# A fused transformer block on one core: weight tiles split, first loads spread, and chunk 0's sum over shifts moved from TensorE to VectorE

## The chip, the cores and the metric

The kernel runs on one core of a Trainium2 chip. Its engines are TensorE (PE in the profile; PEld is its weight load), VectorE (DVE), ScalarE (ACT), GpSimd (POOL) and SyncE (SP), which work side by side and wait for each other through semaphores; each takes its instructions in the order in which the program lists them. Loads and stores are issued by SP or ACT and run on the core's DMA engines. SBUF is the on-chip memory, PSUM holds eight banks of 128 x 512 float32 that TensorE writes. The metric is the time of one execution on the device in microseconds (us).

## The reference

One pre-norm block over 2048 tokens of width 512: attention over 8 dilated earlier positions, then a gated feed-forward part with ReLU.

```python
S, D, H, Dh, W, dil, F = 2048, 512, 32, 16, 8, 2, 1376
def attn(x, wqkv, wo):
    q, k, v = split(x @ wqkv)                      # 32 heads of 16
    idx = pos[:, None] - arange(W)[None, :] * dil  # 8 positions, 2 apart
    logits = einsum("bhsd,bhswd->bhsw", q, k[idx]) * Dh ** -0.5
    logits = where(idx >= 0, logits, -1e9)
    o = einsum("bhsw,bhswd->bhsd", softmax(logits), v[idx])
    return o.reshape(B, S, D) @ wo
def ffn(x, Wg, Wu, Wd):
    gate = x @ Wg
    return ((gate * (gate > 0)) * (x @ Wu)) @ Wd
h   = x + attn(layernorm(x))
out = h + ffn(layernorm(h))
```

## The kernel before

The tokens go through in four chunks of 512 (`tk`). Activations are kept transposed (feature on the partitions), so that a matmul takes weights as its stationary side and 512 tokens as its moving side.

For each chunk:

- layer norm: statistics (`xst`, L432, and `xag`, L435, on VectorE), inverse root by Ln and Exp on ScalarE (L445, L449), scaling (`xxn`: L472 on VectorE in chunk 0, L469 on ScalarE in chunks 1 to 3), transposes on TensorE (`xtp`, L479), copied from a bank by ScalarE (`xte`, L491);
- projections: 12 groups of four matmuls for q, k and v (`qkv0` to `qkv11`, L523), each evicted by ScalarE into `qT`, `kT` or `vT` (L531). In chunk 0 the first two groups are cut into halves of 256 tokens, so that they can start when half of the transposes are there;
- scores: VectorE multiplies q with four shifted views of k at a time (`pr`, L570, 128 x 4096 elements), TensorE sums over the features of a head with the 0/1 matrix `sel` (`sc`, L576), ScalarE takes the exponential (`ex`, L585), in chunk 0 VectorE masks the first positions (`mk`, L588);
- weights: TensorE spreads the eight exponentials over the features with `spread` (`bc`, L604), ScalarE evicts the eight (`be`, L611); the denominator goes through L618, Ln (L621) and Exp (L624);
- weighted sum: for each of four feature tiles VectorE multiplies the eight weights with eight shifted views of v (`mu`, L641, 128 x 4096), then the eight shifts are summed. In the chunks of `PESUM`, which is chunk 0 alone, TensorE does it: eight matmuls with the identity that accumulate in a bank (`ac`, L657), and VectorE scales from the bank (`om`, L661). In the other chunks VectorE adds in a tree of three steps of 2048, 1024 and 512 elements (`tree`, L644) and scales from SBUF (`om`, L648);
- output projection (`wo`, L679), residual and row sums on VectorE (`rs`, L684), second layer norm (L417, L423, L472, L479, L491);
- feed-forward: 22 groups of four matmuls for up and gate (`mm`, L706), evicted by ScalarE (`ue`, L710, and `ge`, L713), multiplied by VectorE (`gu`, L726), then 44 matmuls down (`dn`, L738), the residual (`o`, L742) and a store of 128 KB for each of four row blocks (`os`, L745).

Loads come first, in `setup`: x of chunk 0 in four tiles of 128 KB, two on SP's queue and two on ACT's; then, all on SP's queue, three column blocks of `wqkv` into one tile `wqkv_sb`, x of chunk 1, and the other weights. While they run, 42 matmuls on zeros (`NWARM`, L501) keep TensorE at work.

The order of all other work is set when the program is built. `Plan` collects steps with an engine, an assumed duration, what they wait for and the buffers they take, and `order` lists them: for each engine it finds the steps that could start first, and among those within 0.02 us of the earliest it takes the one with the lowest number in the table `PRIO` (one number for each kind of step and chunk). Steps of all four chunks compete, so projections of later chunks fill TensorE while VectorE works on an earlier one. The order is fixed then; on the chip an instruction only waits for what it needs. The whole x, q, k and hidden tiles share nine buffers (`quad`), products five (`big`), and all matmul outputs eight banks.

Of the kernel before, what the change touches and what calls it, by code (L numbers as in the profile page):

```python
# [8 lines left out]
P = 128  # L9
BF16 = mybir.dt.bfloat16  # L10
# [8 lines left out]
    "warm": (1781, 0, 0, 0),  # L19
    "xst": (1203, 746, 745, 1415),  # L20
    "xag": (-282, 1949, -30, 1438),
    "xrl": (1793, 1763, 1382, 1315),
    "xre": (-53, 1440, 163, 1147),
    "xxn": (801, 1624, 1811, 770),
    "xtp": (-311, 1713, 1279, 573),
    "xte": (-262, -229, 650, 168),
    "qkh0": (1179, 0, 0, 0),
    "qkv0": (397, 1785, 1908, 1357),
    "qe0": (1681, 1220, 1006, 2030),
    "qkh1": (1937, 0, 0, 0),  # L30
    "qkv1": (-27, 1273, 1437, 1309),
    "qe1": (1158, 1502, 1711, 1742),
    "qkv2": (1063, -98, 1193, 1055),
    "qe2": (781, 1293, 1295, 228),
    "qkv3": (732, 1300, 1292, 1219),
    "qe3": (1047, 1347, 1124, 896),
    "qkv4": (1595, 1124, 1549, 240),
    "qe4": (1361, 1357, 882, 377),
    "qkv5": (1414, 1504, 884, 1956),
    "qe5": (354, -58, 1194, 1406),  # L40
    "qkv6": (-356, 1429, 1321, 596),
    "qe6": (996, 1730, 953, 1406),
    "qkv7": (734, 1117, 606, 1375),
    "qe7": (-77, 202, 746, 1484),
    "qkv8": (1584, 1310, 2037, 1115),
    "qe8": (1117, 1084, 1067, 376),
    "qkv9": (711, 23, 593, 938),
    "qe9": (932, 1014, 1152, 1138),
    "qkv10": (1375, 756, 1239, 1096),
    "qe10": (-230, 1252, 1734, 1733),  # L50
    "qkv11": (1671, 1280, 1609, 1967),
    "qe11": (17, 943, 1110, 1362),
    "pr0": (-254, 1165, 1607, 1958),
    "sc0": (-324, 876, 1138, 1287),
    "ex0": (756, 972, 1285, 1085),
    "mk0": (547, 0, 0, 0),
    "pr1": (-47, 530, 999, 2004),
    "sc1": (617, 73, 326, 1774),
    "ex1": (372, 1285, 758, 1130),
    "mk1": (1051, 0, 0, 0),  # L60
    "bc0": (1062, 1244, 1300, 1122),
    "be0": (1138, 1158, 1341, 1095),
    "bc1": (42, 1057, 699, 929),
    "be1": (36, 1684, 1111, 1258),
    "den": (1604, 689, -310, 821),
    "dl": (1791, 1275, 1907, 595),
    "dr": (1335, 1273, 1312, 1699),
    "mu0": (-164, -38, 1183, 1122),
    "ac0": (56, 0, 0, 0),
    "om0": (1093, 1067, 1357, 1300),  # L70
    "mu1": (146, 1353, 1431, 1276),
    "ac1": (1364, 0, 0, 0),
    "om1": (687, 1400, 5, 1302),
    "mu2": (996, 993, 161, 1313),
    "ac2": (-37, 0, 0, 0),
    "om2": (785, 1737, 229, 1404),
    "mu3": (1280, 1240, 1405, 5),
    "ac3": (1975, 0, 0, 0),
    "om3": (1495, 1120, 1180, 231),
    "wo0": (228, 1102, 202, -356),  # L80
    "rs0": (1574, 927, -330, 1158),
    "wo1": (1121, 432, -275, 1193),
    "rs1": (1304, 181, -310, 593),
    "wo2": (-108, -249, 1343, 1034),
    "rs2": (1102, 163, 1048, 1339),
    "wo3": (1179, 946, 1316, 167),
    "rs3": (1309, 1400, 693, 397),
    "hnm": (-250, 1262, 1176, 1363),
    "hsq": (244, 1092, 14, 765),
    "hrl": (1322, 1782, 205, -102),  # L90
    "hre": (1117, 239, 1257, 1320),
    "hxn": (192, 17, 162, 1698),
    "htp": (1031, 1241, 533, 327),
    "hte": (2061, 57, 1584, 1212),
    "mm0": (1870, 1327, 1049, 757),
    "ue0": (1213, 766, -307, 1776),
    "ge0": (1785, -53, 998, 568),
    "gu0": (98, 592, 1451, 1946),
    "mm1": (1000, 1132, 1013, 1247),
    "ue1": (6, 374, 1115, 1933),  # L100
    "ge1": (635, 1100, 1018, 226),
    "gu1": (989, 1213, 146, 931),
    "mm2": (1019, -16, 1051, 872),
    "ue2": (1353, 1361, 1035, 904),
    "ge2": (1251, 1286, 793, 688),
    "gu2": (1674, 1276, 742, 1268),
    "mm3": (1242, 927, 374, 100),
    "ue3": (785, 1698, 41, 1846),
    "ge3": (991, 1869, 1151, 1243),
    "gu3": (1285, 1286, 1272, 1933),  # L110
    "mm4": (1260, 676, 54, 888),
    "ue4": (1, 902, 18, 940),
    "ge4": (1049, 146, 1335, 318),
    "gu4": (1374, 1154, 856, 885),
    "mm5": (1780, 1419, 1193, 1736),
    "ue5": (759, 76, 1742, -129),
    "ge5": (1330, 1083, 1583, 1674),
    "gu5": (1092, -159, 1003, 1066),
    "dn0": (1353, 675, 769, 1954),
    "o0": (-141, 1183, 625, 1829),  # L120
    "os0": (979, 146, 1064, 721),
    "dn1": (901, 1303, 1923, 1112),
    "o1": (1389, 1184, 1790, 188),
    "os1": (1494, 1548, -366, 994),
    "dn2": (1232, 1130, 1287, 1315),
    "o2": (1101, 851, 1278, 1314),
    "os2": (616, 850, 2, 961),
    "dn3": (1208, 1778, 1237, 1152),
    "o3": (743, 1756, 401, 205),
    "os3": (754, 1354, 604, 1066),  # L130
    "xnb": (0, -102, -111, -87),
    "tree0": (0, 621, 196, -129),
# [664 lines left out]
```

## Time and profile before

| | us |
|---|---|
| median of three runs (217.9, 217.58, 216.07) | 217.58 |
| the profiled execution | 216.77 |
| its span in the trace | 215.0 |
| warm-up matmuls, first to last | 0.99 to 5.26 |
| first transposes | 6.59 to 8.02 |
| last matmul ends | 211.66 |
| ScalarE busy | 140.9 |
| one projection or feed-forward group's eviction on ScalarE (L531), mean | 0.60 |
| copy of two transposed row blocks on ScalarE (L491), mean | 1.03 |

The span goes from the first to the last recorded instruction. A group's mean duration can be longer than the distance from one such instruction to the next, as the engines overlap the end of one with the start of the next: a 512-column matmul has a mean of 0.38 us, but eight follow each other in 1.73 us.

### The profile page before, as it was taken

What the parts mean: (1) busy time and instruction counts of PE and PEld (TensorE: products, weight loads), DVE (VectorE), ACT (ScalarE), POOL (GpSimd) and SP (SyncE); (2) the same over time, 40 slices, a digit from 0 to 9 for tenths busy, and PEclk for the clock granted to TensorE, in tenths of its full rate; (3) what the DMA queues carried; (4) which work ended last, traced back from release to release, by engine and by line L of the source; (5) the groups of instructions that cost most, each with busy time, mean ns of one, the idle gap of its engine ahead of it and who ended that gap; (6) DMA issues with size and microseconds to landing.
All of it is one profiled execution on the core that took longest, in us unless ns stands there. A gap on an engine that the chain in (4) does not pass through costs nothing.

```text
span 215.0 us, 3002 instructions
## 1 busy us (share of the span) xinstructions
PE 205.2 (95%) x1141; PEld 98.4 (46%) x1162; DVE 158.6 (74%) x240; ACT 140.9 (66%) x263; POOL 1.6 (1%) x13
## 2 busy tenths in 40 slices
PE   7499899999999999999999999999999999999993
PEld 7255335544455643444444444445444445444441
DVE  6454995999638999999999999849999536212331
ACT  2539979998798976757549662893666453666400
POOL 3000000000000000000000000000000000000000
PEclk9769999999999999999999999999999999999999
DMA  5999800000000000000002000000000000200011
GB/s 165 357 404 375 269 0 5 2 0 0 3 0 0 0 3 0 0 0 3 26 0 73 3 0 0 0 26 27 0 24 0 0 3 24 73 0 5 24 49 49
DMA packets 8670, 10.71 MB, mean 50 GB/s; under 512 B 496, under 2 KB 7504, under 8 KB 8656
## 3 DMA queue, kind: packets, MB, share of 16 engines
q1 hardware_dynamic: 8368, 10.26, 13.9%
q10 hardware_dynamic: 288, 0.26, 0.4%
q8 instruction: 9, 0.15, 0.3%
q14 instruction: 5, 0.04, 0.1%
HBM read 8.42 MB, written 2.10 MB: 49 GB/s over the span
## 4 chain that ended last, share of the span: by engine, by line
PE 91%; DMA 3%; ACT 2%; issue 1%; SPq 1%; DVE 0%; ACTq 0%
PE bank L706 35%; PE bank L523 21%; PE bank L738 18%; PE bank L679 6%; PE bank L576 4%; DMA wqkv_sb<-in_A_wqkv_dram 3%; PE bank L657 3%; PE bank L479 3%; PE bank L604 1%; ACT quad L491 1%; PE bank L618 1%; SPq L342 0%; ACT row L469 0%; DVE row L742 0%; ACT gr L713 0%
## 5 line engine op out<-in xcount | busy, mean ns | idle before, releaser
L523 PE MATMUL bank<-quad,wqkv_sb 128*128 128x512 bf16 (+1 forms) x193 | 45.9, 387 | 2.3 <-DMA wqkv_sb<-in_A_wqkv_dram 1.2
L706 PE MATMUL bank<-quad,wg_sb 128*128 128x512 bf16 (+1 forms) x175 | 45.0, 379 | 0.1
L706 PE MATMUL bank<-quad,wu_sb 128*128 128x512 bf16 (+1 forms) x171 | 44.6, 379 | 0.2
L641 DVE TENSOR_TENSOR big<-big,vT 128x4096 bf16<-128x4096 bf16 x16 | 36.1, 2284 | 6.1 <-ACT big L611 3.9
L738 PE MATMUL bank<-wd_sb,gT 128*128 128x512 bf16 (+1 forms) x170 | 39.2, 379 | 0.3
L570 DVE TENSOR_TENSOR big<-quad,kT 128x4096 bf16<-128x4096 bf16 x16 | 36.0, 2282 | 0.7 <-ACT quad L531 0.7
L710 ACT CAST up_sb<-bank 128x512 bf16<-128x512 f32 (+1 forms) x44 | 25.5, 590 | 15.4 <-PE bank L706 10.9
L713 ACT ACTIVATE gr<-bank 128x512 bf16<-128x512 f32 (+1 forms) x44 | 26.0, 598 | 14.7 <-PE bank L706 10.8
L523 PEld LDWEIGHTS <-wqkv_sb 128*128 128x128 bf16 x200 | 22.4, 117 | 23.7 <-issue 6.8
L706 PEld LDWEIGHTS <-wu_sb 128*128 128x128 bf16 (+1 forms) x176 | 17.5, 100 | 20.6 <-issue 0.4
L726 DVE TENSOR_TENSOR gT<-gr,up_sb 128x1024 bf16<-128x1024 bf16 (+1 forms) x24 | 15.2, 642 | 15.8 <-ACT gr L713 15.4
L706 PEld LDWEIGHTS <-wg_sb 128*128 128x128 bf16 (+1 forms) x176 | 17.3, 100 | 20.9 <-issue 1.5
L738 PEld LDWEIGHTS <-gT 128*128 128x128 bf16 (+1 forms) x176 | 16.8, 98 | 20.5 <-issue 0.7
L644 DVE TENSOR_TENSOR big<-big 128x2048 bf16<-128x2048 bf16 (+2 forms) x36 | 25.9, 772 | 0.0
L491 ACT COPY quad<-bank 128x1024 bf16<-128x1024 bf16 x16 | 16.0, 1025 | 6.1 <-PE bank L479 6.1
L742 DVE TENSOR_TENSOR row<-x_sm,bank 128x512 bf16<-128x512 bf16 x16 | 10.9, 684 | 11.7 <-PE bank L738 11.1
L611 ACT CAST big<-bank 128x512 bf16<-128x512 f32 x32 | 17.6, 605 | 2.7 <-PE bank L604 2.7
L423 ACT ACTIVATE row<-x_sm,mv 128x512 bf16<-128x512 bf16 x16 | 11.4, 716 | 6.7 <-DVE mv L417 6.6
L684 DVE SCALAR_TENSOR_TENSOR x_sm<-x_sm,bank 128x512 bf16<-128x512 bf16 x16 | 10.9, 685 | 6.3 <-PE bank L679 6.0
L679 PE MATMUL bank<-wo_sb,quad 128*128 128x512 bf16 x63 | 15.1, 379 | 0.1
L531 ACT CAST quad<-bank 128x512 bf16<-128x512 f32 x16 | 9.6, 598 | 5.6 <-PE bank L523 5.6
L432 DVE BATCH_NORM_STATS2 st<-x_sm 128x6 f32<-128x512 bf16 x16 | 10.1, 674 | 4.2 <-DMA x_sm<-in_A_x_dram 4.2
(53 smaller groups left out, 133.6 us busy)
## 6 DMA issues: line engine op xcount, KB each, us to landing
out_dram<-row SPq DMA_DIRECT2D x16, 128.0 KB, 1.7
wqkv_sb<-in_A_wqkv_dram SPq DMA_DIRECT2D x3, 512.0 KB, 6.2
x_sm<-in_A_x_dram SPq DMA_DIRECT2D x3, 512.0 KB, 14.0
wu_sb<-in_B_W_up_dram SPq DMA_DIRECT2D x1, 1376.0 KB, 10.8
wg_sb<-in_B_W_gate_dram SPq DMA_DIRECT2D x1, 1376.0 KB, 14.5
wd_sb<-in_B_W_down_dram SPq DMA_DIRECT2D x1, 1280.0 KB, 14.1
wo_sb<-in_A_wo_dram SPq DMA_DIRECT2D x1, 512.0 KB, 8.8
x_sm<-in_A_x_dram ACTq DMA_DIRECT2D x2, 128.0 KB, 2.9
```

Of the source, the lines that this page charges most:

```text
L491: nc.scalar.copy(out=dst.t[:, :, j0 * P:(j0 + n) * P], in_=i)
L523: nc.tensor.matmul(mm.t[:, lo:hi], lhsT=wqkv_sb[:, dt, c * D + t:(c + 1) * D:NT], rhs=xnT.t[:, dt, lo:hi], start=(dt == 0), stop=(dt == NT ...
L570: V.tensor_tensor(out=pb.t[:].rearrange("p (t w) s -> p t w s", t=2), in0=q4, in1=k4, op=ALU.mult)
L611: nc.scalar.copy(out=ab.t[:, w, :], in_=bc.t[:])
L641: V.tensor_tensor(out=mt.t[:], in0=ab.t[:], in1=v8, op=ALU.mult)
L644: V.tensor_tensor(out=mt.t[:, 0:n, :], in0=mt.t[:, 0:n, :], in1=mt.t[:, n:2 * n, :], op=ALU.add)
L679: nc.tensor.matmul(od.t[:], lhsT=OT.t[:, t, j * P:(j + 1) * P], rhs=wo_sb[:, t, :], start=(t == 0), stop=(t == NT - 1))
L706: nc.tensor.matmul(mm.t[:fs, :], lhsT=w_sb[:, dt, ft * P: ft * P + fs], rhs=hnT.t[:, dt, :], start=(dt == 0), stop=(dt == NT - 1))
L710: nc.scalar.copy(out=ub.t[:fs, i, :], in_=um.t[:fs, :])
L713: nc.scalar.activation(out=gr.t[:fs, i, :], in_=gm.t[:fs, :], func=ACT.Relu)
L726: V.tensor_tensor(out=gt.t[:fs, 0:n, :], in0=gr.t[:fs, 0:n, :], in1=ub.t[:fs, 0:n, :], op=ALU.mult)
L738: nc.tensor.matmul(od.t[:], lhsT=gts[ft].t[:fs, ft % 2, j * P:(j + 1) * P], rhs=wd_sb[:fs, ft, :], start=(ft == 0), stop=(ft == NFT - 1))
```

## The change

- The three column blocks of `wqkv` get tiles of their own, `wq_sb`, `wk_sb` and `wv_sb`. x of chunk 0 comes in two loads of 256 KB, one on each queue; then q on SP's queue, k on ACT's, v on SP's.
- `PESUM` is empty: the tree on VectorE sums the shifts in all four chunks.
- In chunk 0 the second half of the transposes is copied from its bank by VectorE instead of ScalarE.
- 54 warm-up matmuls instead of 42.
- In `order` the stretch within which a weightier step may be taken is 0.05 us for TensorE, 0.3 for VectorE and 0.1 for ScalarE instead of 0.02, and all of `PRIO` is replaced; assumed landing times of q, k and v change a little.
- A branch that transposes by DMA is added for the chunks in `DMAT`, of which there are none.

```diff
-    "mu0": (-164, -38, 1183, 1122),
-    "ac0": (56, 0, 0, 0),
+    "mu0": (-490, -741, -300, -559),
+    "tree0": (-169, -269, -240, -508),
...
+    LOOK = {"PE": 0.05, "DVE": 0.3, "ACT": 0.1}
...
-                    ((t, op) for t, op in cands if t <= first + 0.02),
+                    ((t, op) for t, op in cands if t <= first + self.LOOK.get(eng, 0.02)),
...
-    wqkv_sb = sb.tile([P, NT, 3 * D], BF16, name="wqkv_sb")
+    w3_sb = [sb.tile([P, NT, D], BF16, name=f"w{n}_sb") for n in "qkv"]
...
-        wq_r = A_wqkv.rearrange("(dt p) f -> p dt f", p=P)
-        nc.sync.dma_start(x_sm[:, 0:1, :], x_rows[:, 0:1, :])
-        nc.scalar.dma_start(x_sm[:, 1:2, :], x_rows[:, 1:2, :])
-        nc.sync.dma_start(x_sm[:, 2:3, :], x_rows[:, 2:3, :])
-        nc.scalar.dma_start(x_sm[:, 3:4, :], x_rows[:, 3:4, :])
-        for c in range(3):
-            nc.sync.dma_start(wqkv_sb[:, :, c * D:(c + 1) * D], wq_r[:, :, c * D:(c + 1) * D])
+        w3_r = A_wqkv.rearrange("(dt p) f -> p dt f", p=P)
+        nc.sync.dma_start(x_sm[:, 0:2, :], x_rows[:, 0:2, :])
+        nc.scalar.dma_start(x_sm[:, 2:4, :], x_rows[:, 2:4, :])
+        for c, q in enumerate((nc.sync, nc.scalar, nc.sync)):
+            q.dma_start(w3_sb[c][:], w3_r[:, :, c * D:(c + 1) * D])
         nc.sync.dma_start(x_sm[:, BPC:2 * BPC, :], x_rows[:, BPC:2 * BPC, :])
...
-    PESUM = (0,)
-    NWARM = 42
+    PESUM = ()
+    NWARM = 54
+    DMAT = ()
...
-             (("q", 6.0), ("k", 7.5), ("v", 9.0), ("o", 12.5), ("u", 16.5), ("g", 20.5), ("d", 28.0))}
+             (("q", 5.7), ("k", 7.0), ("v", 8.5), ("o", 12.5), ("u", 16.5), ("g", 20.5), ("d", 28.0))}
...
+                tev = not residual and tk == 0 and j0 > 0
...
+                    if tev:
+                        V.tensor_copy(out=o, in_=i)
+                    else:
+                        nc.scalar.copy(out=o, in_=i)
...
-                    nc.tensor.matmul(mm.t[:, lo:hi], lhsT=wqkv_sb[:, dt, c * D + t:(c + 1) * D:NT],
+                    nc.tensor.matmul(mm.t[:, lo:hi], lhsT=w3_sb[c][:, dt, t:D:NT],
...
-            if tk in PESUM:
+            if (tk, t) in PESUM:
```

Lines of the changed kernel are numbered otherwise: L429 and L432 are the statistics, L487 the scaling, L510 and L512 the copies of the transposes by VectorE and ScalarE, L552 the evictions of the projections, L591 the score products, L606 the exponentials, L632 the eviction of the weights, L662 the weighted products, L665 the tree, L669 the scaling after it, L705 the residual.

VectorE at the start of the program, before (`st` and `mv` hold the statistics, `row` a scaled row block):

```order
L432 BN_STATS st_113<-x_sm 128x6
L432 BN_STATS st_114<-x_sm 128x6
L435 BN_AGGR mv_117<-st_113 128x2
L432 BN_STATS st_115<-x_sm 128x6
L435 BN_AGGR mv_117<-st_114 128x2
L432 BN_STATS st_116<-x_sm 128x6
L435 BN_AGGR mv_117<-st_115 128x2
L435 BN_AGGR mv_117<-st_116 128x2
L472 TENSOR_SCALAR row_104<-x_sm,mv_117,rs_129 128x512
```

VectorE at the same place after the change, from the last statistics of chunk 0 to the first of chunk 1:

```order
L429 BN_STATS st_118<-x_sm 128x6
L432 BN_AGGR mv_119<-st_118 128x2
L487 TENSOR_SCALAR row_106<-x_sm,mv_119,rs_131 128x512
L487 TENSOR_SCALAR row_107<-x_sm,mv_119,rs_131 128x512
L487 TENSOR_SCALAR row_108<-x_sm,mv_119,rs_131 128x512
L487 TENSOR_SCALAR row_109<-x_sm,mv_119,rs_131 128x512
L510 COPY quad_80<-bank_137 128x4x256
L429 BN_STATS st_115<-x_sm 128x6
```

All four statistics still stand ahead of the first scaling; the copy of the second half is new on VectorE and stands ahead of chunk 1's statistics.

VectorE from chunk 0's weighted products on, before (`big` the products, `vT` and `kT` the values and keys, `bank` PSUM, `rec` the inverse denominators):

```order
L641 TENSOR_TENSOR big_87<-big_91,vT 128x4096
L453 SCALAR_TENSOR_TENSOR nb_126<-mv_120,rs_131 128x4
L641 TENSOR_TENSOR big_88<-big_91,vT 128x4096
L453 SCALAR_TENSOR_TENSOR nb_127<-mv_119,rs_132 128x4
L641 TENSOR_TENSOR big_89<-big_91,vT 128x4096
L641 TENSOR_TENSOR big_90<-big_91,vT 128x4096
L570 TENSOR_TENSOR big_87<-quad_81,kT 128x4096
L570 TENSOR_TENSOR big_88<-quad_81,kT 128x4096
L661 TENSOR_TENSOR quad_84<-bank_137,rec_103 128x512
L661 TENSOR_TENSOR quad_84<-bank_136,rec_103 128x512
```

The same place after the change:

```order
L662 TENSOR_TENSOR big_89<-big_93,vT 128x4096
L450 SCALAR_TENSOR_TENSOR nb_128<-mv_122,rs_133 128x4
L662 TENSOR_TENSOR big_90<-big_93,vT 128x4096
L662 TENSOR_TENSOR big_91<-big_93,vT 128x4096
L665 TENSOR_TENSOR big_90<-big_90 128x2048
L665 TENSOR_TENSOR big_90<-big_90 128x1024
L665 TENSOR_TENSOR big_90<-big_90 128x512
L662 TENSOR_TENSOR big_92<-big_93,vT 128x4096
L432 BN_AGGR mv_121<-st_118 128x2
L665 TENSOR_TENSOR big_89<-big_89 128x2048
L665 TENSOR_TENSOR big_89<-big_89 128x1024
```

Where chunk 1's score products followed the four weighted products, the trees of chunk 0 stand now; the score products come behind them.

ScalarE around the eviction of chunk 0's weights, before (`ex` the exponentials, `big_91` the weights):

```order
L585 ACTIVATE ex_100<-bank_135 128x512
L531 CAST vT<-bank_136 128x512
L611 CAST big_91<-bank_140 128x512
L611 CAST big_91<-bank_133 128x512
L531 CAST kT<-bank_138 128x512
L611 CAST big_91<-bank_134 128x512
L611 CAST big_91<-bank_135 128x512
L611 CAST big_91<-bank_136 128x512
L611 CAST big_91<-bank_140 128x512
L611 CAST big_91<-bank_133 128x512
L531 CAST vT<-bank_134 128x512
L611 CAST big_91<-bank_139 128x512
```

The same place after the change (`big_93` the weights):

```order
L606 ACTIVATE ex_102<-bank_142 128x512
L632 CAST big_93<-bank_139 128x512
L632 CAST big_93<-bank_140 128x512
L632 CAST big_93<-bank_136 128x512
L632 CAST big_93<-bank_141 128x512
L632 CAST big_93<-bank_135 128x512
L632 CAST big_93<-bank_142 128x512
L632 CAST big_93<-bank_139 128x512
L632 CAST big_93<-bank_140 128x512
L442 ACTIVATE rs_133<-mv_122,eps_t 128x4
```

Three evictions of projections stood between the exponential and the last of the eight; now the eight follow the exponential in one run.

249 lines of the change are left out of this document (130 added, 119 removed).

## The prediction

> **What bounds the kernel now.** I read the page first, then the chain of work that ended last, the groups by line, the timeline of TensorE and of VectorE over the first 100 us, and last the windows and the waits of VectorE.
>
> The page: its first line, TensorE's busy line, and the chain by engine; behind them, from the groups by line, the one that the change removes and the scaling that takes over for another (columns: line, engine, operation, count; busy us, mean ns; idle before).
>
> ```profile
> span 215.0 us, 3002 instructions
> PE 205.2 (95%) x1141; PEld 98.4 (46%) x1162; DVE 158.6 (74%) x240; ACT 140.9 (66%) x263; POOL 1.6 (1%) x13
> PE 91%; DMA 3%; ACT 2%; issue 1%; SPq 1%; DVE 0%; ACTq 0%
> L657 PE MATMUL bank<-big,identity 128*128 128x512 bf16 x31 | 7.5, 379 | 0.1
> ...
> L648 DVE TENSOR_TENSOR quad<-big,rec 128x512 bf16<-128x512 bf16 x12 | 4.9, 417 | 0.0
> ```
>
> TensorE is busy 95% of the span and is 91% of the chain. VectorE's 74% is a mean: by stage it is much fuller, as the windows below show. So work taken off TensorE shortens the span one for one only as long as VectorE does not fall behind it.
>
> The chain in order of time (start, length, what): the weights' load, eight of the matmuls that sum over shifts, the first output projection of chunk 1, the last VectorE step.
>
> ```profile
> 2.66 7.20 DMA wqkv_sb<-in_A_wqkv_dram
> ...
> 41.40 1.73 PE bank L657 x8
> ...
> 98.14 0.86 PE bank L679 x4
> ...
> 211.68 0.69 DVE row L742
> ```
>
> **Part 1, the sum over shifts in chunk 0.** The 32 matmuls of L657 go; eight take 1.73, so TensorE loses 32 x 0.216 = 6.9 us, all of it on the chain. VectorE takes over four trees of three adds. These rows of its timeline give the pitch of each step as the distance to the next row:
>
> ```profile
> 40.34 4.48 DVE L641 TENSOR_TENSOR big<-big,vT 128x4096 bf16<-128x4096 bf16 x2
> 44.74 4.48 DVE L570 TENSOR_TENSOR big<-quad,kT 128x4096 bf16<-128x4096 bf16 x2
> 49.14 1.88 DVE L661 TENSOR_TENSOR quad<-bank,rec 128x512 bf16<-128x512 f32 x3
> ...
> 71.01 4.23 DVE L644 TENSOR_TENSOR big<-big 128x2048 bf16<-128x2048 bf16 x6
> 75.15 4.49 DVE L570 TENSOR_TENSOR big<-quad,kT 128x4096 bf16<-128x4096 bf16 x2
> ```
>
> A product is (44.74 - 40.34) / 2 = 2.20; a tree is (75.15 - 71.01) / 2 = 2.07. The scaling that follows takes 0.42 from SBUF (L648 above), some 0.34 of it at the pitch of a full engine, where it was about 0.6 from a bank (three in 1.88). Net on VectorE: 4 x 2.07 - 4 x 0.27 = +7.2 us, all in chunk 0. The copy that evicts the second half of the first transposes also moves to VectorE (part 2).
>
> **Part 2, the start.** VectorE's rows of the first 14 us, then TensorE's (start, length, engine, line, operation, operands, count; in brackets the idle time before and what ended it):
>
> ```profile
> 3.41 1.29 DVE L432 BATCH_NORM_STATS2 st<-x_sm 128x6 f32<-128x512 bf16 x2 [0.42 <-DMA x_sm<-in_A_x_dram]
> ...
> 6.15 1.42 DVE L472 TENSOR_SCALAR row<-x_sm,mv,rs 128x512 bf16<-128x512 bf16 x4
> 11.38 2.47 DVE L432 BATCH_NORM_STATS2 st<-x_sm 128x6 f32<-128x512 bf16 x4 [3.81 <-DMA x_sm<-in_A_x_dram]
> ```
> ```profile
> 8.41 0.37 PE L523 MATMUL bank<-quad,wqkv_sb 128*128 128x256 bf16 x1 [0.39 <-ACT quad L491]
> 10.00 2.08 PE L523 MATMUL bank<-quad,wqkv_sb 128*128 128x256 bf16 x8 [1.22 <-DMA wqkv_sb<-in_A_wqkv_dram]
> ```
>
> One projection matmul ran at 8.41, as soon as its activations were there; the second waited until the third load of the shared tile landed (2.66 + 7.20 = 9.86). With a tile for each of q, k and v that wait goes, and the activations are late next. They will themselves be later: x comes as two loads of 256 KB instead of four of 128 KB, one per queue. The queues' loads run side by side; this is a window over both (the stretch, then each engine's busy time, the granted clock, the share of the DMA engines, GB/s):
>
> ```profile
> 2.00:4.00 2.00, 2.00 (x22) 2.00 (x20) 1.52 (x7) 0.94 (x1) 0.25 (x3) 1.00 0.83 276
> ```
>
> The last column is GB/s: about 0.55 MB moved by 4.0, which is just over the 0.52 MB of chunk 0's x, whose bytes are through by 3.9. A pair on each queue therefore lands near 4.2, where a single tile landed at 3.41. From the first statistics to the scaling took 6.15 - 3.41 = 2.74, and from there to the first projection 2.26; so the first projection comes at 4.2 + 2.74 + 2.26 = 9.2, say 9.3 since the order puts all four statistics ahead of the scaling in both. Bounds: 8.5 (the pair lands at 3.5) and 10.0 (nothing gained); 9.3 is nearest to what the bytes allow. Against 10.0, less the 0.1 of work that was done at 8.41: -0.6. The second half's copy on VectorE has no row; bounds are a 128x512 step from a bank, 0.6, and twice that. It is hidden: it ends near 10.1 while TensorE has eight half-width matmuls from 9.3, and VectorE's next work, chunk 1's statistics, waits for x until 11.38 as before. The k load's issue on ACT's queue (0.4 to 0.6 us) sits ahead of the table load, and ACT's first work is at 5.5: nothing. Twelve more warm-up matmuls end before the transposes, which now start near 7.4: nothing on the path.
>
> The Trainium skill, "DMA: Bandwidth & Descriptors", section "Issuing engines are not separate DMA queues", says that loads issued from different engines run on the same 16 DMA engines and interleave. The window above agrees with it: 276 GB/s with both queues loaded, no more than the 372 to 402 of the later windows below, where SP's queue ran alone. Were the queues independent, the SP pair alone would land near 3.5, the first projection would come at 8.5, and the sum would be 0.8 lower.
>
> The clock: these windows show it (granted clock in the last column but two).
>
> ```profile
> 8.02:10.00 1.98, 0.38 (x2) 0.03 (x1) 0.00 (x0) 1.25 (x2) 0.00 (x0) 0.52 1.10 372
> 10.00:14.90 4.90, 4.67 (x19) 2.80 (x21) 2.75 (x8) 1.17 (x2) 0.00 (x0) 0.50 1.04 402
> 14.90:20.00 5.10, 5.10 (x25) 2.71 (x24) 0.92 (x2) 4.09 (x9) 0.00 (x0) 1.00 1.04 389
> ```
>
> TensorE had 0.38 us of work in the 2 us to 10.0, the clock fell to half, and 4.67 us of work then ran at half: 2.3 lost. The idle stretch now shrinks to some 0.5 us. Bounds for the loss: 0, if the clock never falls, and 2.8, if it still returns only at 14.9 (half of 14.9 - 9.3). I take 1.1, a return about two microseconds after the start, between them and nearer the low end because the gap that brought the clock down is mostly gone: -1.2. The Trainium skill, "TensorE: Matmul & The Clock Gate", Part 1, says that the clock is set by activity in free-running windows of about 3.4 us; the 6.9 us from 8.0 to 14.9 are two of them. By that rule a start that fills too little of its window would keep half clock until 14.9, and the sum would be 1.7 higher.
>
> **Part 3, what VectorE's extra work does.** TensorE can go on without chunk 0's sums for long, as it has other chunks' projections; the order keeps them ahead of the first output projections. What ends last is VectorE's way to chunk 1's last scaling, for which chunk 1's first output projection (98.14 before) waits. VectorE's rows of that way, and its windows (second number of each pair of columns is the count; DVE busy is the third group), with its two largest waits:
>
> ```profile
> 19.24 8.90 DVE L570 TENSOR_TENSOR big<-quad,kT 128x4096 bf16<-128x4096 bf16 x4 [0.66 <-ACT quad L531]
> ...
> 35.78 2.29 DVE L641 TENSOR_TENSOR big<-big,vT 128x4096 bf16<-128x4096 bf16 x1 [2.19 <-issue]
> ...
> 96.60 0.41 DVE L648 TENSOR_TENSOR quad<-big,rec 128x512 bf16<-128x512 bf16 x1
> ```
> ```profile
> 35.78:57.53 21.75, 21.50 (x138) 10.03 (x140) 20.24 (x14) 20.24 (x37) 0.00 (x0) 1.00 0.01 2
> 57.53:65.31 7.78, 7.73 (x44) 3.90 (x44) 3.16 (x13) 6.52 (x15) 0.00 (x0) 1.00 0.00 0
> 65.31:97.01 31.70, 31.45 (x179) 14.54 (x180) 31.45 (x34) 24.14 (x46) 0.00 (x0) 1.00 0.00 1
> ```
> ```profile
> DVE big L641 <- ACT big L611: 3.9, 1, 3.9
> DVE x_sm L684 <- PE bank L679: 2.3, 4, 1.5
> ```
>
> Before, from the first weighted product (35.78) to chunk 1's last scaling (97.01) VectorE worked 20.2 + 3.2 + 31.5 = 54.9 and waited 6.4, almost all of it in the two waits shown. Now two things change besides the work.
>
> It starts earlier. The order evicts q0, k0, q1, k1 first, with no v among them, so the first score product needs four groups of projections (16 x 0.216 = 3.5, plus 1.1 for the clock, plus 0.7 for the eviction): 9.3 + 5.3 = 14.6, behind chunk 1's statistics (11.38 + 2.47 = 13.9, and the last of its aggregates), say 14.8 instead of 19.24. Four of them end near 23.6 instead of 28.1. From there to the first weighted product it was 35.78 - 28.1 = 7.7; the order now lets ACT run the eight weight evictions in one go (five took 2.63, so 4.3 for eight), so I take 7.4: 31.0.
>
> It has more to do. The order has from the first weighted product to chunk 1's last scaling 17 products (37.4), 8 trees (16.6), 8 scalings (2.7), 4 residual steps of 0.7 (2.8), and 3.4 of small ones: 62.9. And the two waits are covered now: a score product stands between chunk 0's sums and the residual steps, and eight score products instead of four stand ahead of chunk 1's weighted products. I leave 1.0 of the 6.4 (bounds 0 and 6.4). So 31.0 + 62.9 + 1.0 = 94.9.
>
> TensorE without new waits would be there earlier. Ahead of that place stand 32 sums less, but 4 projections, 8 narrow score matmuls and 2 denominators more (1.8 in all, no longer behind it): 98.14 - 6.9 + 1.8 - 0.6 - 1.2 = 91.2. So VectorE makes TensorE wait 94.9 - 91.2 = 3.7 us somewhere from 30 to 95, where before it hardly waited. That is the price of the 7.2 us of added work after the 4.8 us of earlier start.
>
> Behind that place VectorE has room (before, it was busy 79.0 of 113.5 there), so TensorE runs as it did:
>
> ```profile
> 98.14:211.66 113.52, 112.92 (x577) 52.12 (x586) 78.98 (x126) 64.99 (x123) 0.00 (x0) 1.00 0.06 18
> ```
>
> 94.9 + 113.5 - 1.8 = 206.6 for TensorE's end. The tail was 215.0 - 211.7 = 3.3. The order finishes the last four row blocks three matmuls (0.65 us) apart, so four stores of 128 KB crowd; bounds 0 and one store's 1.7 us to landing; I take 0.3.
>
> **The sum.** 215.0 - 6.9 - 0.6 - 1.2 + 3.7 + 0.3 = 210.3 of span; by the place, 206.6 + 3.6 = 210.2. The profiled execution took 216.77 with a span of 215.0, so 1.8 lies around it: 212.0. Its 216.77 stands 0.8 below the median 217.58 of the runs.
>
> The rule that an engine may be held a few tenths of a microsecond for a weightier step acts when the program is built; on the chip it is only an order, and is in the places above.
>
> **Rivals.**
> - VectorE keeps up: its start is early enough and TensorE waits nowhere anew. For it: 4.8 earlier against 7.2 more is nearly even, and chunk 0's products may leave earlier than I have it. Against: 31.45 busy of 31.70 before. 91.2 + 111.7 + 3.6 + 1.8 = 208.3.
> - The two waits stay: VectorE again waits 6.4. For it: ACT was 20.24 of 21.75 busy while chunk 0's weighted products ran. 31.0 + 62.9 + 6.4 = 100.3, then + 111.7 + 3.6 + 1.8 = 217.4: no change.
> - The new tiles don't bring the start forward: x or q lands late, the first projection comes at 10.0 and half clock lasts to 14.9. Then both engines are 1.8 later: 213.8. By the clock rule of the Trainium skill above, this is where an unlucky window would end.
> - Slower: ACT sets VectorE's pace in chunk 0, as its 93% there says, so that the added 7.2 to 8.4 us (with the copy's 1.2) lie wholly on VectorE's way to chunk 1's last scaling: 97.0 + 8.4 = 105.4, and 105.4 + 111.7 + 5.4 = 222.5. It decides if the first weighted product stays near 35.8; the time is over 1% longer once chunk 1's output projection starts after 102.7 (219.8 - 117.1).
>
> **Chances.** Forecast 0.55 (210 to 215), VectorE keeps up 0.20, late start 0.06, waits stay 0.12, slower 0.07. A change of less than about 1% (2.2 us) can't be told from none here. Faster by over 1%: 0.55 + 0.20 + 0.06 = 0.81; within 1%: 0.12; slower: 0.07. The range goes from 207.3, the first rival with no loss to the clock (208.3 - 1.1, rounded up), to 216.8, just short of the waits that stay.
>
> **What would show it.** No TensorE group on identity and big; the first projections near 9.3 without a wait on a weight load; score products from about 14.8 and weighted products from about 31; VectorE without gaps over 1 us from there to 95; new TensorE waits on VectorE of 3 to 4 us before chunk 1's output projection near 95, and none after. It is wrong if weighted products still start at 35, if TensorE waits behind 100, or if the tail grows by over 1 us.

## The result, and the profile after

| | us, median (lowest to highest) | ratio to the kernel before, 95% interval |
|---|---|---|
| kernel before | 217.03 (216.07 to 217.9) | |
| changed kernel | 211.06 (210.98 to 211.27) | 0.9727, 0.9679 to 0.9776 |

The changed kernel is 2.7% faster. Its profiled execution took 211.08 us with a span of 209.3, where the prediction had 212.0 and 210.3.

The page of the changed kernel: TensorE's and the other engines' busy time, and the chain that ended last by engine.

```profile
span 209.3 us, 2987 instructions
...
PE 199.4 (95%) x1142; PEld 96.7 (46%) x1142; DVE 169.6 (81%) x253; ACT 137.7 (66%) x262; POOL 1.6 (1%) x13
...
PE 69%; DVE 24%; issue 2%; ACT 2%; DMA 2%; DVEq 0%; ACTq 0%
```

TensorE lost 205.2 - 199.4 = 5.8 us of busy time and VectorE gained 11.0. The chain shows what this did: VectorE was 0% of it and is 24% now. It runs over VectorE with few breaks from the first weighted product (29.09) to the last of the score products near 73 us, and over TensorE alone from there to the last matmul.

Windows of the changed kernel: from the first projection to the first weighted product, on to 50 us, through the stretch of waits, up to chunk 1's output projection, and the rest (columns as in the prediction).

```profile
9.47:29.09 19.62, 18.82 (x131) 9.89 (x131) 18.23 (x32) 16.49 (x32) 0.00 (x0) 1.00 0.83 297
29.09:50.00 20.91, 19.99 (x115) 10.74 (x113) 20.53 (x24) 19.60 (x38) 0.00 (x0) 1.00 0.01 2
50.00:74.33 24.33, 21.70 (x167) 9.39 (x165) 23.62 (x26) 21.00 (x43) 0.00 (x0) 1.00 0.00 1
74.33:93.86 19.53, 19.53 (x91) 9.06 (x92) 19.32 (x22) 11.87 (x23) 0.00 (x0) 1.00 0.00 1
93.86:205.85 111.99, 111.98 (x574) 50.92 (x572) 80.75 (x129) 65.43 (x124) 0.00 (x0) 1.00 0.05 16
```

The granted clock is 1.00 from the first projection on. From there on TensorE idles only ahead of 74.33: 0.80 + 0.92 + 2.63 = 4.35 us in the first three windows. The next view, the waits of TensorE from 9 to 100 us (what waited for what: us, times, longest), says for whom.

```profile
PE bank L597 <- DVE big L591: 2.5, 3, 0.9
PE bank L544 <- ACT quad L512: 1.4, 3, 0.8
PE bank L700 <- DVE quad L669: 0.4, 1, 0.4
```

The largest new waits are for VectorE's score products (L591), 2.5 us. Of the 1.4 for ScalarE's copies of the transposes (L512), 0.39 lies ahead of the first projection and 0.8 at 24.6. Chunk 1's output projection, where I had expected VectorE to end last, does not wait at all (the 0.4 at L700 is chunk 0's, at 48.79): TensorE has been held back before, and comes to it at 93.86, while VectorE does the last two scalings (93.62 to 94.37). TensorE's part of the chain (start, length, what):

```profile
74.33 19.10 PE bank L727 x88
...
93.86 3.55 PE bank L700 x16
```

VectorE's timeline at the places that the prediction timed: chunk 1's first statistic, the first score product, the first weighted product, two trees of chunk 0, the last scalings of chunk 1.

```profile
10.47 0.69 DVE L429 BATCH_NORM_STATS2 st<-x_sm 128x6 f32<-128x512 bf16 x1 [0.66 <-DMA x_sm<-in_A_x_dram]
...
13.84 2.29 DVE L591 TENSOR_TENSOR big<-quad,kT 128x4096 bf16<-128x4096 bf16 x1
...
29.09 2.29 DVE L662 TENSOR_TENSOR big<-big,vT 128x4096 bf16<-128x4096 bf16 x1
...
35.77 2.41 DVE L665 TENSOR_TENSOR big<-big 128x2048 bf16<-128x2048 bf16 x3
38.09 2.28 DVE L662 TENSOR_TENSOR big<-big,vT 128x4096 bf16<-128x4096 bf16 x1
...
93.62 0.75 DVE L669 TENSOR_TENSOR quad<-big,rec 128x512 bf16<-128x512 bf16 x2
```

TensorE's timeline at the start:

```profile
3.73 3.19 PE L522 MATMUL bank<-warm 128*128 128x128 bf16 x28
7.65 1.43 PE L494 MATMUL bank<-identity,row 128*128 128x128 bf16 x16 [0.73 <-DVE row L487]
9.47 0.60 PE L544 MATMUL bank<-quad,wq_sb 128*128 128x256 bf16 x4 [0.39 <-ACT quad L512]
```

No wait on a weight load is left at the first projections; they come at 9.47, and the gap ahead of the transposes is 0.73 us.

### The profile page after: what moved, and what is told of

The parts are those of the page before. It is cut to its first block, busy times and chain, and to the rows that moved or that the text cites. A ratio compares the mean times of both kernels' runs of the same rounds, so it can differ in the third digit from the quotient of the medians.

```text
span 209.3 us, 2987 instructions
## 1 busy us (share of the span) xinstructions
PE 199.4 (95%) x1142; PEld 96.7 (46%) x1142; DVE 169.6 (81%) x253; ACT 137.7 (66%) x262; POOL 1.6 (1%) x13
## 4 chain that ended last, share of the span: by engine, by line
PE 69%; DVE 24%; issue 2%; ACT 2%; DMA 2%; DVEq 0%; ACTq 0%
PE bank L727 36%; PE bank L759 18%; DVE big L591 8%; PE bank L700 5%; PE bank L544 5%; DVE big L665 4%; DVE big L662 4%; DVE st L429 3%; PE bank L494 2%; PE bank L597 2%; DMA x_sm<-in_A_x_dram 2%; DVE x_sm L705 1%; ACT quad L512 1%; DVE row L487 1%; DVE mv L432 1%
## 5 line engine op out<-in xcount | busy, mean ns | idle before, releaser
L727 PE MATMUL bank<-quad,wu_sb 128*128 128x512 bf16 (+1 forms) x176 | 45.2, 379 | 0.0
L759 PE MATMUL bank<-wd_sb,gT 128*128 128x512 bf16 (+1 forms) x176 | 40.5, 379 | 0.0
L665 DVE TENSOR_TENSOR big<-big 128x2048 bf16<-128x2048 bf16 (+2 forms) x48 | 37.0, 778 | 1.0
L591 DVE TENSOR_TENSOR big<-quad,kT 128x4096 bf16<-128x4096 bf16 x16 | 36.0, 2288 | 0.8 <-ACT kT L552 0.7
L662 DVE TENSOR_TENSOR big<-big,vT 128x4096 bf16<-128x4096 bf16 x16 | 36.3, 2288 | 0.0
L632 ACT CAST big<-bank 128x512 bf16<-128x512 f32 x32 | 16.6, 626 | 2.3 <-PE bank L625 2.3
L512 ACT COPY quad<-bank 128x1024 bf16<-128x1024 bf16 x15 | 14.8, 1033 | 5.0 <-PE bank L494 5.0
L544 PE MATMUL bank<-quad,wv_sb 128*128 128x512 bf16 x64 | 16.2, 381 | 0.8 <-ACT quad L512 0.8
L544 PE MATMUL bank<-quad,wq_sb 128*128 128x512 bf16 (+1 forms) x68 | 15.7, 366 | 0.6 <-ACT quad L512 0.6
L544 PE MATMUL bank<-quad,wk_sb 128*128 128x512 bf16 (+1 forms) x68 | 15.7, 367 | 0.0
L700 PE MATMUL bank<-wo_sb,quad 128*128 128x512 bf16 x64 | 14.7, 379 | 0.4 <-DVE quad L669 0.4
L597 PE MATMUL bank<-big,sel 128*32 128x512 bf16 x128 | 9.7, 384 | 2.5 <-DVE big L591 2.5
L429 DVE BATCH_NORM_STATS2 st<-x_sm 128x6 f32<-128x512 bf16 x16 | 10.5, 670 | 1.7 <-DMA x_sm<-in_A_x_dram 1.7
```

What stands on the lines that cost most here:

```text
L429: V.bn_stats(out=st.t[:], in_=x_sm[:, tk * BPC + j, :])
L512: nc.scalar.copy(out=o, in_=i)
L544: nc.tensor.matmul(mm.t[:, lo:hi], lhsT=w3_sb[c][:, dt, t:D:NT], rhs=xnT.t[:, dt, lo:hi], start=(dt == 0), stop=(dt == NT - 1))
L591: V.tensor_tensor(out=pb.t[:].rearrange("p (t w) s -> p t w s", t=2), in0=q4, in1=k4, op=ALU.mult)
L632: nc.scalar.copy(out=ab.t[:, w, :], in_=bc.t[:])
L662: V.tensor_tensor(out=mt.t[:], in0=ab.t[:], in1=v8, op=ALU.mult)
```

## The experiments

In the expectations, theory V has VectorE's way to chunk 1's output projection set the end, T has TensorE's own work set it, C is about the clock, O and D about orders; L, S, B and the unnamed rivals are told in the expectation itself. Each ratio is to runs of the kernel before on the same chip, whose medians were 216.8 to 218.0 us. These runs scatter by up to 2.5 us, those of the other kernels by 0.1 to 1.1, so versions that differ by one or two us are compared by their own medians. Nine kernels vary the start, the sums or VectorE's order; two more test what the first nine had left over.

**x of chunk 0 in four loads again**, in the changed kernel:

```diff
-        nc.sync.dma_start(x_sm[:, 0:2, :], x_rows[:, 0:2, :])
-        nc.scalar.dma_start(x_sm[:, 2:4, :], x_rows[:, 2:4, :])
+        nc.sync.dma_start(x_sm[:, 0:1, :], x_rows[:, 0:1, :])
+        nc.scalar.dma_start(x_sm[:, 1:2, :], x_rows[:, 1:2, :])
+        nc.sync.dma_start(x_sm[:, 2:3, :], x_rows[:, 2:3, :])
+        nc.scalar.dma_start(x_sm[:, 3:4, :], x_rows[:, 3:4, :])
```

> The changed kernel with x of chunk 0 in four loads of 128 KB again. Both theories expect the first projection earlier, near 8.6 instead of 9.47, since the first statistics start at 3.4. Theory V (VectorE's way to chunk 1's output projection decides up to 94 us): the loads behind are issued later, x of chunk 1 lands near 11.3 instead of 10.5, the first score product comes near 14.6 instead of 13.84, and the time grows by 0.3 to 0.9 us, to about 211.7. Theory T (TensorE is the bound from the first projection on): the time falls by 0.8 us, to about 210.2.

212.31 us (0.9768, 0.9720 to 0.9816): 1.2 more than the changed kernel, the direction of V and more than the 0.3 to 0.9 that it had. The first statistic came earlier, at 3.35 instead of 4.00, but the loads behind x landed later, and that mattered more. TensorE's and VectorE's rows:

```profile
9.34 0.63 PE L546 MATMUL bank<-quad,wq_sb 128*128 128x256 bf16 x4 [0.90 <-DMA wq_sb<-in_A_wqkv_dram]
```
```profile
12.53 0.69 DVE L431 BATCH_NORM_STATS2 st<-x_sm 128x6 f32<-128x512 bf16 x1 [3.36 <-DMA x_sm<-in_A_x_dram]
...
15.74 2.28 DVE L593 TENSOR_TENSOR big<-quad,kT 128x4096 bf16<-128x4096 bf16 x1
```

The first projection now waited for q's load, so it gained 0.1 instead of the 0.9 that both theories had given it. Chunk 1's x landed 2.1 later, and the first score product came at 15.74 instead of 13.84. A start that TensorE had 0.1 earlier and VectorE 1.9 later cost 1.2. The extra issues explain only a part: q and chunk 1's x were issued 0.4 later, but q took 7.6 us to landing instead of 5.5. From 4 to 5 us the DMA engines moved 150 GB/s here and 384 in the changed kernel; why is open.

**One tile for q, k and v again**, same loads and queues:

```diff
-    w3_sb = [sb.tile([P, NT, D], BF16, name=f"w{n}_sb") for n in "qkv"]
+    wqkv_sb = sb.tile([P, NT, 3 * D], BF16, name="wqkv_sb")
```

> The changed kernel with q, k and v in one tile again, the loads and their queues unchanged. Theory of the prediction (the tile of its own frees the second matmul from the wait on v): the first projections wait for v's load. In the changed kernel v lands at 1.73 + 7.2 = 8.9, ahead of the first projection at 9.47, so by that reading of the trace the split costs and brings nothing: 211.1, within 0.3. If the split itself is what brought the start forward, the first projections come at 10.0 and the time is 211.5 or more.

211.06 us (0.9719, 0.9684 to 0.9754), the same as with three tiles, and its first projection came at 9.46. So the split brings nothing here. The wait went because v landed earlier and the activations came later. In the changed kernel q, k and v were issued at 1.23, 1.25 and 1.73, and the page gives 5.5, 7.0 and 7.2 us to landing. The last, v, was there at 8.9, before the activations at 9.47; the kernel before had its third load at 9.86 and its activations at 8.41. So of the wait about 0.9 went by the earlier landing, and the rest because the activations are 1.1 later. The earlier issue and the second queue were not tested apart.

**42 warm-up matmuls**, in the changed kernel:

```diff
-    NWARM = 54
+    NWARM = 42
```

> The changed kernel with 42 warm-up matmuls instead of 54. They end near 5.3, and 2.3 us without work on TensorE follow before the transposes at 7.65. Theory C (the longer warm-up keeps the clock up): the clock falls to half before the first projections and stays there for two to five us; the first score product moves from 13.8 to between 15 and 17, and the time grows by 1 to 3 us, to 212 to 214. Rival: what kept the clock up is that the first projections don't wait any more; the time stays within 0.3 us of 211.1.

212.4 us (0.9779, 0.9744 to 0.9815), 1.3 more. TensorE's rows of it:

```profile
7.64 1.44 PE L494 MATMUL bank<-identity,row 128*128 128x128 bf16 x16 [2.00 <-DVE row L487]
9.46 1.01 PE L544 MATMUL bank<-quad,wq_sb 128*128 128x256 bf16 x4 [0.38 <-ACT quad L512]
10.27 1.06 PE L544 MATMUL bank<-quad,wk_sb 128*128 128x256 bf16 x4
...
13.19 3.19 PE L544 MATMUL bank<-quad,wk_sb 128*128 128x256 bf16 x16
```

The projections start at the same time, but after a gap of 2.00 us four of them take 0.81 (10.27 - 9.46) where they took 0.44. By the windows the granted clock is still 1.00 while the transposes run, falls at 9.25, 1.6 us after the gap has ended, and is 0.50 until 12.66. The first score product came at 15.38, the first weighted product at 30.63. Theory C held: the twelve extra warm-ups keep the clock up.

**The kernel before with the new start alone** (three tiles, two x loads, both queues, 54 warm-ups; its sums and order), and **the same with its 42 warm-ups**:

> The kernel before, with the three weight tiles, the two loads of x, the queues and 54 warm-up matmuls of the change; sums over shifts and order as before. The prediction's terms for the start alone: 0.6 for the first projection and 1.2 (at most 2.3) for the clock, and VectorE's start moves along: 214.2 to 215.3, against 217.0 of the kernel before. If the start is hidden behind VectorE, it stays within 0.5 of 217.

> The kernel before with the three weight tiles, two x loads and the loads on both queues, but with the 42 warm-up matmuls it had (before_new_start had 54 and took 213.55 us, span 211.9). Sums over shifts and order as before. Theory C (the twelve more warm-ups carry the clock, here as in the changed kernel): the idle stretch before the transposes grows from 0.42 to about 1.6 us, TensorE runs at half clock until about 13 us, and 1.2 to 1.6 are lost: 214.7 to 215.2. Theory L (the earlier loads alone did it; with the first projection at 9.0 the clock stays full without them): 213.3 to 213.8.

213.55 us (0.9811, 0.9754 to 0.9869) and 215.01 us (0.9889, 0.9835 to 0.9944). The start is worth 1.9% and so most of the gain; without the extra warm-ups it is worth 1.1%, as theory C had it. TensorE's rows of the first:

```profile
7.21 1.44 PE L477 MATMUL bank<-identity,row 128*128 128x128 bf16 x16 [0.42 <-DVE row L470]
9.02 0.60 PE L521 MATMUL bank<-quad,wq_sb 128*128 128x256 bf16 x4 [0.38 <-ACT quad L489]
```

and of the second:

```profile
7.45 1.44 PE L477 MATMUL bank<-identity,row 128*128 128x128 bf16 x16 [1.81 <-DVE row L470]
9.28 1.01 PE L521 MATMUL bank<-quad,wq_sb 128*128 128x256 bf16 x4 [0.39 <-ACT quad L489]
```

The first one's span of 211.9 comes out of the prediction's rows: 215.0, less the whole 2.3 us lost at half clock, less about 0.9 for projections that run without a break from 9.02. I had expected 214.2 to 215.3, by the smaller clock term of the prediction. The sum fits, but it rests on one profiled execution of the kernel before (see the clock below).

**The kernel before with the sum moved alone**, and **with start and sum but its old order**:

```diff
-                def f_ac(mt=mt, u=u):
-                    for w in range(W):
-                        nc.tensor.matmul(u.t[:], lhsT=identity[:], rhs=mt.t[:, w, :],
-                                         start=(w == 0), stop=(w == W - 1))
+                def f_ac(mt=mt, u=u, f=f_a):
+                    f(4, mt)
+                    f(2, mt)
+                    V.tensor_tensor(out=u.t[:], in0=mt.t[:, 0, :], in1=mt.t[:, 1, :], op=ALU.add)
```

> The kernel before, with chunk 0's sums over shifts on VectorE and nothing else changed: three adds in place of each eight matmuls, the last add into the bank, in the places that the matmuls had in the order. Theory V: 9.4 us more on VectorE's way, which starts as late as before, against 6.9 less on TensorE: chunk 1's output projection moves from 98 to 104 to 106, and the time is 221 to 224, slower. Theory T: 6.9 less on TensorE, 210 to 212.

> The kernel before with its order kept, but with both edits at once: the new start (three tiles, two x loads, both queues, 54 warm-ups; alone 213.55 us) and chunk 0's sums as three adds on VectorE in the places of the matmuls (alone 227.54 us). What is left of the change is the order alone. Theory O (the order is what makes the move pay: in the old one TensorE stands before chunk 1's score products while VectorE sums, early or not): the parts add, 211.9 + 10.8 = 222.7 of span, 223 to 225 us. Theory S (the earlier start gives VectorE the room that the sums need): VectorE is 3 to 4 us earlier, so most of the 8 us of waits on its score products goes, 214 to 218 us.

227.54 us (1.0454, 1.0402 to 1.0506) and 223.78 us (1.0294, 1.0229 to 1.0358). In both the last add goes into a bank and the scaling reads it there, so VectorE has 10.5 us more to do (four sums of 2.6), where the prediction had 7.2 for the change. This is the largest effect in the study, and it goes the other way: taking 6.9 us off TensorE made the kernel 4.5% slower, more than the 224 us that V had at most. VectorE came to the next score product at 53.36 instead of 44.74, and TensorE, which waited for it, had nothing else to do. TensorE's rows and windows of the kernel with the sum moved alone:

```profile
46.70 0.59 PE L523 MATMUL bank<-quad,wqkv_sb 128*128 128x512 bf16 x1 [4.04 <-ACT quad L491]
...
55.70 1.04 PE L576 MATMUL bank<-big,sel 128*32 128x512 bf16 x8 [7.14 <-DVE big L570]
```
```profile
40.00:52.00 12.00, 3.23 (x19) 1.49 (x21) 11.76 (x12) 9.87 (x16) 0.00 (x0) 0.76 0.00 0
52.00:60.00 8.00, 4.30 (x16) 1.17 (x15) 7.83 (x7) 0.58 (x1) 0.00 (x0) 0.51 0.00 0
```

In 12 us TensorE had 3.2 of work; the clock fell to half and stayed there until 60, for which V had no term. The same stretch of the kernel before shows why the matmuls that went saved next to nothing:

```profile
40.79 0.61 PE L479 MATMUL bank<-identity,row 128*128 128x128 bf16 x8
41.24 1.89 PE L657 MATMUL bank<-big,identity 128*128 128x512 bf16 x8
...
46.87 0.81 PE L523 MATMUL bank<-quad,wqkv_sb 128*128 128x512 bf16 x3
```

The sums (L657) filled just those stretches in which ScalarE scaled and copied for the transposes. With them TensorE came to the next projection at 46.87, without them at 46.70, held there by ScalarE's copy. The run without them was about 0.7 later by then (its first weighted product came at 36.50, not 35.78), so of the 6.9 us of work at most 0.9 was time up to there. The second wait, of 7.14, comes from VectorE's added work. The new start takes off 3.8 us (225.8 to 222.0 of span), about what it takes off alone, and the two waits remain (4.0 and 7.1 in both). So the parts add (expected 222.7), and theory O holds: in the old order the moved sum costs, with the early start or without. Order and sum together, with the copy on VectorE, are worth 2.5 us, the step from 213.55 to 211.06. The new order with all sums left on TensorE was not run, so whether the move has a share in these 2.5, or the order alone brings them, is open.

**One of chunk 0's four tiles summed on TensorE again**, in the changed kernel, with one score product moved ahead of the residual steps:

```diff
+    for w in range(W):
+        nc.tensor.matmul(u[:], lhsT=identity[:], rhs=mt.t[:, w, :], start=(w == 0), stop=(w == W - 1))
```

> The changed kernel with one of chunk 0's four feature tiles summed on TensorE again (eight matmuls in a free bank), and one of chunk 1's score products taken ahead of the residual steps so that VectorE has work meanwhile. TensorE has 1.73 us more, VectorE 2.1 less on the way to chunk 1's output projection. Theory V: TensorE's waits there go, and the time falls by about 1 us, to 209.6 to 210.4. Theory T: it grows by 1.7, to 212.8.

211.02 us (0.9696, 0.9649 to 0.9744): no change, which neither theory had. VectorE's next score product did come 2.2 earlier, at 46.79 instead of 48.99, but then it waited (VectorE's waits from 28 to 95 us):

```profile
DVE big L591 <- ACT kT L552: 1.9, 3, 1.0
DVE big L591 <- ACT quad L552: 0.6, 1, 0.6
```

It had waited 0.7 there. With 1.73 us more on TensorE the projections came later, and ScalarE's evictions with them. So here work handed from VectorE to TensorE moved the wait between the three engines without shortening it. It also means that in the new order this quarter of the sums is worth nothing either way.

**Tree steps of two tiles in turn**, in the changed kernel, chunks 0 and 1. Nothing is added or taken away: the three dependent adds of one tile no longer follow each other directly. In chunk 0 a weighted product and a few small steps change places with them. The lines for chunk 1, where `put` sets named steps into the places that such steps have in the list:

```diff
     todo = plan.order()
+    T = [("tree%d" % t, 1) for t in range(4)]
+    put((323, 328, 331, 333, 337, 341), (T[1], T[0], T[1], T[0], T[1], T[0]))
+    put((354, 359, 362, 364, 366, 368), (T[2], T[3], T[2], T[3], T[2], T[3]))
```

> The changed kernel with the tree steps of two feature tiles taken in turn on VectorE in chunks 0 and 1, no two dependent steps next to each other; TensorE's and ScalarE's order unchanged. Eight trees take 2.07 us each instead of 2.3 to 2.4. Theory V: VectorE reaches chunk 1's last scaling 1.5 to 2 us earlier, TensorE's waits on it shrink by as much, and the time falls to 209.1 to 209.6. Theory T: the trees are off the path but for the waits of 0.4 us at chunk 0's output projection, so the time stays at 210.7 to 211.1.

209.76 us (0.9656, 0.9621 to 0.9691), 1.3 less, the direction of V and close to what it had. VectorE's rows:

```profile
35.88 2.96 DVE L665 TENSOR_TENSOR big<-big 128x2048 bf16<-128x2048 bf16 x3
38.75 2.28 DVE L662 TENSOR_TENSOR big<-big,vT 128x4096 bf16<-128x4096 bf16 x1
...
41.04 2.46 DVE L665 TENSOR_TENSOR big<-big 128x1024 bf16<-128x1024 bf16 x4
...
91.74 0.75 DVE L669 TENSOR_TENSOR quad<-big,rec 128x512 bf16<-128x512 bf16 x2
```

Chunk 1's last scalings came at 91.74 instead of 93.62. The eight trees took 16.6 us by the distances between rows, against 18.4 in the changed kernel. The chain of the changed kernel shows the difference in the first two adds of one tree:

```profile
35.85 1.15 DVE big L665
37.00 0.02 issue
37.03 0.70 DVE big L665
```

Each add starts 0.02 us after the one that it reads has ended. Independent instructions start about 0.09 before the end of the one ahead (a product lasts 2.29 and takes 2.20 in a row). That is 0.1 for each dependent pair.

**Statistics in turn**, and **both orders together**. The same holds for the layer norm's statistics, each of which is followed directly by the aggregate that reads it in the changed kernel, but not in the kernel before:

```diff
     todo = plan.order()
+    for tk, slots in ((0, (12, 13, 14, 15, 16, 19, 20, 21)), (1, (38, 41, 44, 46, 47, 50, 51, 54))):
+        st, ag = ("xst", tk), ("xag", tk)
+        put(slots, (st, st, ag, st, ag, st, ag, ag))
```

> The changed kernel with the statistics of chunks 0 and 1 on VectorE in the order that the kernel before had: each aggregate one statistic later, so that no aggregate follows directly on the statistic that it reads; all else as in the changed kernel. Theory D (a VectorE instruction that reads what the one just before it wrote starts only when that has ended, an independent one about 0.1 us sooner): from the first statistic to the first scaling 2.74 us instead of the 3.21 of the changed kernel, the first projection near 9.05 instead of 9.47, the warm-up gap gone, the first score product near 13.35 instead of 13.84, and 0.3 to 0.5 less at the end: 210.5 to 210.8 us. Rival B (from 50 to 74 us VectorE, TensorE and ScalarE are coupled so that an earlier start of 0.45 is lost in waits): the start moves as in D, but 210.9 to 211.2 us.

> Both orders together: tree steps of two tiles in turn (trees_interleaved, 209.76 us) and the statistics as in stats_interleaved. Theory D: the gains add, 209.2 to 209.5 us. Rival B: VectorE already waits for ScalarE's evictions in trees_interleaved, so nothing more comes: 209.6 to 209.9 us.

210.56 us (0.9703, 0.9667 to 0.9739) and 209.22 us (0.9639, 0.9609 to 0.9669). Theory D held for both, with gains of 0.50 and 0.54; the second is the fastest version of this study. VectorE's rows of the first:

```profile
3.94 1.29 DVE L429 BATCH_NORM_STATS2 st<-x_sm 128x6 f32<-128x512 bf16 x2 [0.95 <-DMA x_sm<-in_A_x_dram]
...
6.68 1.42 DVE L487 TENSOR_SCALAR row<-x_sm,mv,rs 128x512 bf16<-128x512 bf16 x4
...
13.30 2.29 DVE L591 TENSOR_TENSOR big<-quad,kT 128x4096 bf16<-128x4096 bf16 x1
```

From the first statistic to the scaling it is 2.74 again instead of 3.21. The one miss is the gap ahead of the transposes: it grew to 1.42 us instead of closing, because the warm-ups ended sooner: the 54 took 4.72 us there and 5.94 in the changed kernel, at a granted clock of 1.00 in both; why is open. The clock stayed full all the same.

Not tried: the longer stretch for weightier steps by itself, and the copy on VectorE by itself. The order comes out of the rule and the table together, and what each has of the gain stays open.

## Why the prediction was right, and where it was not

The time came out at 211.06 against 212.0, by a better start, a new order with less work on TensorE, and part of it given back where TensorE now waits for VectorE. The shares are not the predicted ones. The start alone gave 3.1 us of span in the profiled executions (215.0 to 211.9), where the prediction had 1.8; sum, order and tail gave 2.6 (211.9 to 209.3), where it had 6.9 - 3.7 - 0.3 = 2.9. By the steps of the prediction:

- **The start, -0.6.** The first projection came at 9.47 (predicted 9.3). The loads landed at 4.0, 0.2 before the estimate, but statistic to scaling took 3.21, since I carried 2.74 over from an order without dependent pairs. Cause and effect were mixed up in one point: I gave the tiles the credit for the vanished wait, and with one tile it is gone too.
- **The clock, -1.2: mis-sized, and its cause misread.** I took half of the loss of 2.3 to remain. None did in the changed kernel: the granted clock was 1.00 from the first projection on. I had put the fall down to the two idle microseconds before 10.0. Windows of the kernel before show that the clock had fallen at their start, at about 8.1:

```profile
8.00:9.00 1.00, 0.40 (x2) 0.00 (x0) 0.00 (x0) 1.00 (x2) 0.00 (x0) 0.55 1.10 385
9.00:10.00 1.00, 0.00 (x0) 0.03 (x1) 0.00 (x0) 0.27 (x1) 0.00 (x0) 0.50 1.11 361
...
14.00:15.00 1.00, 1.00 (x7) 0.72 (x5) 0.13 (x2) 0.59 (x1) 0.00 (x0) 0.53 1.03 405
```

What lies before it is the gap of 1.34 between the warm-ups and the transposes. So what I had taken for nothing on the path, the extra warm-ups, is what decides: without them the changed kernel is 1.3 slower. That the kernel before loses its whole 2.3 to the clock is not shown. In 5 of the 28 runs of it beside the experiments the mean granted clock is 1.00, and their spans (214.3 to 216.7) are no shorter than those of the 20 runs with 0.984, the profiled execution's value (214.5 to 216.3). No trace of them was kept, and why is open.
- **VectorE starts earlier.** The first score product came at 13.84 (14.8), mostly by the clock, and because chunk 1's x, issued at 2.27 instead of 3.21, landed 0.9 sooner. The first weighted product came at 29.09 (31.0): from the end of the products it took 6.3, not 7.4.
- **VectorE's work, 62.9: mis-sized.** From 29.09 to the end of chunk 1's last scalings at 94.3 it was 65.2 less the 0.7 of its wait there, 64.5. The 1.6 more are the trees: I took 2.07 for each, from a row in which two trees stood in turn, and they took 2.3 because their steps now follow each other directly.
- **The new waits, +3.7.** With full clock and the first projection at 9.47, TensorE alone would have reached chunk 1's output projection at 91.2 - 1.1 + 0.2 = 90.3; it was there at 93.86, so 3.6 were lost. The size is right and the place is not: the waits lie before 74 us, at the score products, and about 1.0 of them is for ScalarE's copies, which the prediction did not have. The size is luck in part, as VectorE's earlier start (1.9) and its longer trees (1.6) nearly cancel.
- **Behind it.** TensorE took 111.99 (111.7), the tail 3.45 (3.6).
- **The sum over shifts, -6.9.** I called all of it on the chain. But the chain could not show that in the old order these matmuls filled waits: moved alone, they gave +10. The prediction's 91.2 rested on the new order's filling the place, which I took from the order and did not price. The total of sum and waits came out near its size; that the move itself has a part in it is not shown, and one tile of four handed back changed nothing.

So the terms that missed are a clock term 1.1 too small, which is about what the span came out shorter (209.3 against 210.3), VectorE's trees 1.6 to 1.8 too short, and VectorE's start 1.9 too late. The rivals that kept VectorE's waits or let it fall further behind did not come; that it would keep up did not come either, though it does in part once the dependent steps are taken apart.

## What to carry to other kernels

Taking a matmul off the chain saves its time only if something else can run in its place: before work is moved off a busy engine, look at what its neighbours in the queue wait for, and move the order with the work. When VectorE becomes the bound, put independent instructions between a result and its reader before moving work again. A start is cheap to improve: earlier issue of the loads that are waited for, and enough warm-up work to come close to the first real matmul.

## What the runs showed of the hardware

- **Dependent VectorE instructions.** A reader directly behind its writer starts some 0.02 us after the writer's end, an independent instruction about 0.09 before it. Taking the pairs apart in 8 trees and 8 statistics saved 1.84 us (211.06 to 209.22) without one instruction less. The Trainium skill, "VectorE: DVE Perf Modes", section "The DRAIN you can't avoid", says that the next operation does not start until the pipeline is empty, and that one that is not held starts earlier. The trace agrees for a reader behind its writer (0.02 after the end), and independent instructions do start earlier here (0.09 before the end).
- **The clock and short gaps.** The granted clock fell to half at 9.25 and came back at 12.66 with 42 warm-ups in the changed kernel, at 8.98 and 12.39 with the new start and 42, at 8.10 and 14.93 in the kernel before, and at 46.16 and 59.84 with the sum moved alone: half speed for 3.4, 3.4, 6.8 and 13.7 us, so one, two and four times the same stretch. The gap ahead of the transposes does not decide by its length alone. After 0.42 and 0.73 the clock stayed full and after 1.81 and 2.00 it fell, but 1.34 us came before a fall in the kernel before and before none in the fastest version. The Trainium skill, "TensorE: Matmul & The Clock Gate", Part 1, gives free-running windows of about 3.4 us, an idle one of which lowers the clock. The stretches at half speed agree with whole windows; the gaps that came before a fall at the start are shorter than one.
